# K and V of two heads in one transfer, and batches of eight heads, in a decode-attention block on one core

## The chip, the core and the metric

The kernel runs on one core of a Trainium2 chip. A core has a matrix engine (TensorE, PE in the profile), a vector engine (VectorE, DVE), an activation engine (ScalarE, ACT), GpSimd (POOL), SyncE (SP), which here only issues transfers, and 16 DMA engines that move data between the chip's memory (HBM) and the on-chip buffer (SBUF). Matrix products land in PSUM, of which the kernel uses eight banks of 512 float32 columns on 128 partitions. The metric is the device time of one execution in microseconds; the median of three runs is compared.

## What is computed

One decode step of a transformer block: four sequences (B = 4), one new token each, width D = 576, 32 query heads over 16 heads of K and V (two query heads share one), head size 128, and a cache of 16,384 tokens of which only the last 4,096 are attended to. Everything is bfloat16.

```python
q = (layernorm(x) @ wq)                        # (4, 1, 32 heads, 128)
k = k_cache[:, :, Sk - W:, :]                  # (4, 16, 4096, 128), each head used by 2 query heads
v = v_cache[:, :, Sk - W:, :]
p = softmax(einsum("bhqd,bhkd->bhqk", q, k) * Dh ** -0.5)
h = x + einsum("bhqk,bhkd->bhqd", p, v).reshape(B, 1, Hq * Dh) @ wo
gate, up = layernorm(h) @ W_gate, layernorm(h) @ W_up      # 576 x 4608 each
out = h + (gate * (gate > 0) * up) @ W_down                # 4608 x 576
```

The windows of K and V are 4 x 16 x 1 MB each, 134 MB together; the weights (wq, wo, gate, up, down) are some 25 MB.

## The kernel before

The work of each engine is written out by hand as a list of instructions, one list per engine, and the lists are tied together by semaphores (a small class, `Sched`, counts them). `S.op` and `S.dma` first wait for the named events in `deps` and then issue, so an engine never overtakes its own list. The unit of the attention part is one head of K and V of one sequence, 64 in all, numbered i.

**Transfers.** `prog_sync` is SyncE's list: it goes through `transfers` in order, waits until the target is free, and issues. The order is wq (five transfers), then K(i) with V(i - 5) behind it, then wo, gate and up, down, and last the output. K and V are 1 MB each. A head's window of 4,096 tokens is laid out as 128 rows of 32 consecutive tokens, one row of 8,192 bytes for each partition:

```python
return cache[b, kvh, SK - WIN:SK, :].rearrange("(p t) d -> p (t d)", p=128)
```

They go into slots of `pool`: a ring of six for K (`add_K`, the transfer at line 200) and of ten for V (`add_V`, line 203). A K slot comes free when VectorE has transposed that head (event TR), a V slot when PE has done its PV matmuls.

**Scores.** VectorE transposes each K head with 32 x 32 blocks (`tr`, line 382) from the slot into one of three `kT` buffers. PE's `qk(i)` then does eight matmuls of 512 columns into two PSUM banks; its weights `qz` hold q for the four heads of a batch in such a way that the four heads accumulate into different rows of the same two banks. Batches (four heads, 16 of them) alternate between two pairs of banks, so the scores are double-buffered.

**Softmax of a batch.** VectorE takes the row maxima (`rmax`, lines 385 and 387), GpSimd combines them over the partitions (PARTITION_ALL_REDUCE, line 268), VectorE makes the bias (`fbias`, lines 392 and 394), ScalarE takes the exponential with sums (line 314), VectorE transposes the result (`trp`, line 398), and ScalarE casts it into `prob` (line 321). In VectorE's list, `fbias` and `trp` of a batch stand behind the first and second transposes of the next batch.

**PV.** `pv(j)` is six heads behind `qk` in PE's list: eight matmuls of 512 columns with eight weight columns (four token groups times two query heads). After four heads ScalarE copies the bank out (`cpy`, line 301), and PE's `ext` picks the wanted blocks with four small matmuls. `norm` divides by the sums once for each sequence.

**The rest.** The output projection with wo, the second layernorm, gate and up, and down follow as the weights land; the wo transfers reuse K slots, gate and up V slots, and the down weights wait for the end of the output projection. All matmuls are recorded by one helper at line 469 (`mm`), so they share that line in the profile.

Of the kernel before, what the change touches and what calls it, by code (L numbers as in the profile page):

```python
# [19 lines left out]
T = WIN // 128  # L20
# [3 lines left out]
NPAIR = B * KVH  # L24
NB = 4
NBATCH = NPAIR // NB
# [3 lines left out]
SLOT = 4608  # L30
NKS = 6
NVS = 10
NSLOT = NKS + NVS
# [3 lines left out]
PVLAG = 6  # L37
# [63 lines left out]
def bass_sequential_preLN__sliding_block_cached__glu_gated_reglu__decode_kernel(  # L101
# [12 lines left out]
    with ExitStack() as es:  # L114
# [4 lines left out]

        pool = sb("pool", [128, NSLOT, SLOT], BF16)  # L120
        kT = sb("kT", [128, NKT, WIN // 2], FP32)
# [20 lines left out]
        mask = sb("mask", [128, 4, 2 * NB], FP32)  # L142
        selT = sb("selT", [128, 4, 2 * NB], FP32)
        rmx = sb("rmx", [128, 2], FP32)
        pmax = sb("pmax", [128, 2, 2 * NB], FP32)
        bcm = sb("bcm", [128, 2, 2 * NB], FP32)
        t8 = sb("t8", [128, 2 * NB], FP32)
        bias = sb("bias", [128, 2], FP32)
        rs2 = sb("rs2", [128, 2, 2], FP32)
# [3 lines left out]
        prob = sb("prob", [128, 3, NB, T, 2], BF16)  # L153
# [13 lines left out]
        sc = [es.enter_context(nc.psum_tensor(f"sc{i}", [128, 1024], FP32)) for i in range(2)]  # L167
        pb = [sc[0][:, 0:512], sc[0][:, 512:1024], sc[1][:, 0:512], sc[1][:, 512:1024]]
# [7 lines left out]

        rings = {"K": [list(range(NKS)), 0], "V": [list(range(NKS, NSLOT)), 0]}
        slot_user = {}
        transfers = []
        slot_of = {}  # L180

        def add(name, ring, consumer, make, fixed=None):
            if ring is not None:
                slots, i = rings[ring]
                s = slots[i % len(slots)]
                rings[ring][1] += 1
                free = slot_user.get(s)
                slot_user[s] = consumer
                key = f"slot{s}"
            else:  # L190
                s, free, key = fixed, None, "fix_" + str(name).replace("'", "").replace("(", "").replace(")", "").replace(", ", "_")
            slot_of[name] = s
            transfers.append((name, key, free, lambda e, s=s: make(e, s)))

        def kv(cache, i):
            b, kvh = divmod(i, KVH)
            return cache[b, kvh, SK - WIN:SK, :].rearrange("(p t) d -> p (t d)", p=128)

        def add_K(i):
            add(("K", i), "K", ("TR", i), lambda e, s: e.dma_start(out=pool[:, s, 0:WIN], in_=kv(A_k_cache, i)))  # L200

        def add_V(i):
            add(("V", i), "V", ("PV", i), lambda e, s: e.dma_start(out=pool[:, s, 0:WIN], in_=kv(A_v_cache, i)))

        for c in range(4):
            add(("wq", c), "V", "QMM", lambda e, s, c=c: e.dma_start(out=pool[:, s, 0:H * DH], in_=A_wq[c * 128:(c + 1) * 128, :]))
        add(("wq", 4), "V", "QMM", lambda e, s: e.dma_start(out=pool[:, s, 0:H * DH // 2],
                                                            in_=A_wq[512:576, :].rearrange("r (u n) -> (r u) n", u=2)))
        for m in range(NPAIR + VLEAD):
            if m < NPAIR:  # L210
                add_K(m)
            if m >= VLEAD:
                add_V(m - VLEAD)
        for g in range(NWO):
            add(("wo", g), "K", "ATTN",
                lambda e, s, g=g: e.dma_start(out=pool[:, s, :].rearrange("p (q x) -> p q x", q=2),  # L216
                                              in_=A_wo[g * 1024:(g + 1) * 1024, :].rearrange("(q p e) n -> p q (e n)", q=2, e=4)))
        for c in range(4):
            for kind, W in (("wg", B_W_gate), ("wu", B_W_up)):
                add((kind, c), "V", None,  # L220
                    lambda e, s, c=c, W=W: e.dma_start(out=pool[:, s, 0:F], in_=W[c * 128:(c + 1) * 128, :]))

        s4 = rings["V"][0][rings["V"][1] % NVS]
        for u, (kind, W) in enumerate((("wg", B_W_gate), ("wu", B_W_up))):
            transfers.append(((kind, 4), f"gu4_{u}", slot_user[s4],
                              lambda e, u=u, W=W: e.dma_start(out=pool[:, s4, u * HALF:(u + 1) * HALF],
                                                              in_=W[512:576, :].rearrange("r (u n) -> (r u) n", u=2))))
        wd_sb = pool[:, 0:NKS, :].rearrange("p s x -> p (s x)")[:, 0:FC * D].rearrange("p (g x) -> p g x", g=NG)
        WD = [(0, GD * JJ), (GD * JJ, 2 * GD * JJ)] + [(g * JJ, (g + 1) * JJ) for g in range(2 * GD, NG - 1)] + [(FC - JJ, FC - 1), (FC - 1, FC)]
        for k, (f0, f1) in enumerate(WD):  # L230
            g0, j0 = divmod(f0, JJ)
            g1, nj = (f1 // JJ, JJ) if f1 - f0 >= JJ else (g0 + 1, f1 - f0)
            transfers.append((("wd", k), f"wd{k}", "ATTN",
                              lambda e, g0=g0, g1=g1, j0=j0, nj=nj: e.dma_start(
                                  out=wd_sb[:, g0:g1, j0 * D:(j0 + nj) * D],
                                  in_=B_W_down[g0 * 128 * JJ:g1 * 128 * JJ, :].rearrange("(g p j) n -> p g (j n)", p=128, j=JJ)[:, :, j0 * D:(j0 + nj) * D])))
# [5 lines left out]
        def prog_sync(S):  # L242
            for name, key, free, make in transfers:
                S.dma("sync", make, key, deps=[free], name=land(name))
# [5 lines left out]
        def prog_pool(S):  # L250
# [12 lines left out]
                 deps=["P1"], name="IDF")  # L263
            for n in range(NBATCH):
# [7 lines left out]
        def prog_act(S):  # L272
# [12 lines left out]
            def qzero(n):  # L285
                b, q = divmod(n, 4)
                for g in range(4):
                    deps = []
                    if g == 0:
                        deps = ["D_QR", "QZ0"] if n < 2 else [("QK", NB * (n - 2) + NB - 1)]  # L290
                    src = bass.AP(tensor=qrep, offset=32 * g * 4 * H * B + 8 * q * B + b, ap=[[4 * H * B, 32], [2 * B, NB], [H * B, 4], [B, 2]])
# [13 lines left out]
            for n in range(NBATCH):  # L305
                for half in range(2):
                    deps = []
                    if half == 0:
# [5 lines left out]
                    S.op(a, lambda e, n=n, half=half: e.activation(  # L314
                        out=P[:, half * 512:(half + 1) * 512], in_=sc[n % 2][:, half * 512:(half + 1) * 512], func=ACT.Exp,
                        scale=SCALE, bias=bias[:, n % 2:n % 2 + 1], accum_out=rs2[:, n % 2, half:half + 1]),
                        deps=deps, name=("EXP", n) if half else None, signal=half == 1)
                deps = [("TRP", n)]
                if n >= 3:
                    deps.append(("PV", NB * (n - 3) + NB - 1))  # L320
                S.op(a, lambda e, n=n: e.copy(out=prob[:, n % 3, :, :, :],  # L321
                                              in_=probT[:, :, 0:2 * NB].rearrange("p t (r h) -> p r t h", h=2)), deps=deps, name=("CMP", n))
# [13 lines left out]
        def prog_dve(S):  # L336
# [17 lines left out]
            for x in range(2):  # L354
                S.op(v, lambda e, x=x: e.memset(pb[PVB + x], 0.0), name=f"PVZ{x}")  # L355
            S.op(v, lambda e: e.tensor_reduce(out=mask[:, 0, :], in_=ident_b[:, :].rearrange("p (r u) -> p u r", u=2 * NB), axis=AX.X, op=ALU.add),
                 name="M0")
            S.op(v, lambda e: e.tensor_reduce(out=mask[:, 3, :], in_=bass.AP(tensor=ident_b, offset=0, ap=[[128, 128], [1, 2 * NB], [32, 4]]),
                                              axis=AX.X, op=ALU.add), name="M3")
            S.op(v, lambda e: e.tensor_scalar(out=mask[:, 1, :], in0=mask[:, 0, :], scalar1=2 * BIG, scalar2=-BIG, op0=ALU.mult, op1=ALU.add),  # L360
                 deps=["M0"], name="M1")
            S.op(v, lambda e: e.tensor_scalar(out=mask[:, 2, :], in0=mask[:, 0, :], scalar1=-2 * BIG, scalar2=BIG, op0=ALU.mult, op1=ALU.add),
                 name="M2")
            S.op(v, lambda e: e.reciprocal(out=st1[:, 5:6], in_=st1[:, 4:5]), deps=["A_STD"], name="D5")
# [11 lines left out]
            def tr(i):  # L376
                deps = [land(("K", i))]
                if i >= NKT:
                    deps.append(("QK", i - NKT))
                src = pool[:, slot_of[("K", i)], 0:WIN].bitcast(FP32).rearrange("p (t c k) -> p c t k", c=2, k=32)  # L380
# [3 lines left out]
            def rmax(n):  # L384
                S.op(v, lambda e: e.tensor_reduce(out=rmx[:, n % 2:n % 2 + 1], in_=sc[n % 2][:, :], axis=AX.X, op=ALU.max),  # L385
                     deps=[("QK", NB * n + NB - 1)], name=("RMAX", n))
# [4 lines left out]
            def fbias(n):  # L391
                S.op(v, lambda e: e.scalar_tensor_tensor(out=t8[:, :], in0=bcm[:, n % 2, :], scalar=-SCALE, in1=mask[:, 2, :],  # L392
                                                         op0=ALU.mult, op1=ALU.max), deps=[("PAR", n)], name=("T8", n))
                S.op(v, lambda e: e.tensor_reduce(out=bias[:, n % 2:n % 2 + 1], in_=t8[:, :], axis=AX.X, op=ALU.min),  # L394
                     deps=[("T8", n)] + ([("EXP", n - 2)] if n >= 2 else []), name=("BIAS", n))

            def trp(n):
                S.op(v, lambda e: e.transpose(out=probT[:, :, :].rearrange("p t j -> p (t j)"), in_=P[:, :]),  # L398
                     deps=[("EXP", n)] + ([("CMP", n - 1)] if n >= 1 else []), name=("TRP", n))
                b, q = divmod(n, 4)  # L400
                S.op(v, lambda e: e.tensor_tensor(out=rs1[:, n % 2:n % 2 + 1], in0=rs2[:, n % 2, 0:1], in1=rs2[:, n % 2, 1:2], op=ALU.add),  # L401
                     name=("RS1", n))
                S.op(v, lambda e: e.tensor_scalar(out=rowsum[:, b, 8 * q:8 * q + 8], in0=mask[:, 3, :], scalar1=rs1[:, n % 2:n % 2 + 1],
                                                  scalar2=None, op0=ALU.mult), deps=[("RS1", n)], name=("RSUM", n))

            def norm(b):
# [3 lines left out]
                     deps=[("RS", b), ("EXT", 4 * b + 3)], name=("NORM", b))  # L410

            for i in range(NPAIR):
                tr(i)
                if i == 0:
                    S.op(v, lambda e: e.tensor_copy(out=qT_sb[:, :], in_=pb[QB][:, 0:H * B]), deps=["QMM"], name="D_QT")
                    S.op(v, lambda e: e.tensor_copy(out=qrep[:, :, :].rearrange("p c x -> p (c x)"), in_=pb[QR]), deps=["QREP"], name="D_QR")  # L416
                    S.op(v, lambda e: e.tensor_copy(out=selT[:, :, :].rearrange("p t (r h) -> p t r h", h=2),
# [224 lines left out]
```

## Time and profile before

| | |
|---|---|
| median of 3 runs | 389.65 us (389.43 to 389.69) |
| the profiled execution | 389.34 us, span 387.6 us |
| PE busy | 301.1 us, 78% of the span |
| VectorE (DVE) busy | 204.6 us, 53% |
| ScalarE (ACT) busy | 60.1 us, 16% |
| GpSimd (POOL) busy | 10.7 us, 3% |
| moved by the DMA queues | 159.88 MB, mean 413 GB/s |
| K transfers, issue to landing (median) | 26.1 us |
| V transfers, issue to landing (median) | 26.9 us |

The profile is one execution on the chip, recorded by hardware; its times are microseconds unless marked ns. The span is the time from the first to the last instruction. A page has a strip of 40 equal slices of the span, where a digit is the busy share in tenths; the row DMA is the mean over the 16 engines, and GB/s is what they moved. The queue lines give packets, megabytes and the share of 16 engines' span; the lines of issues give the tile and its source, the issuing queue, the number and size of the transfers and the median time from issue to landing. The chain that ended last follows the last instruction back to what released it. A group of instructions has its line, engine, operation, what it writes and reads, its shapes and its count; behind the first bar the busy time and the mean duration in ns, behind the second the idle time of the engine before them and what ended it.

### The profile page before, as it was taken

The page shows a single profiled execution, that of the slowest core. Times are in us where ns is not written, and L with a number is a line of the kernel's source. Part 1 is how long each engine was busy: PE and PEld are TensorE (multiplying, and loading weights), DVE is VectorE, ACT ScalarE, POOL GpSimd, SP SyncE. Part 2 cuts the span into 40 slices and gives each one's busy share as a digit, 9 for nine tenths or more (in the row PEclk, how much of TensorE's full clock was granted, in tenths as well). Part 3 has the DMA queues.
Part 4 walks back from the last instruction along what each step waited for, and adds up shares of the span by engine and source line. Part 5 has one row for each costly group of instructions (what it writes and reads, how often), then busy time and mean ns, then how long its engine had stood idle before and what let it go on. Part 6 is the DMA issues. An engine that isn't in the chain of part 4 may idle for free.

```text
span 387.6 us, 4471 instructions
## 1 busy us (share of the span) xinstructions
PE 301.1 (78%) x1906; PEld 131.3 (34%) x1906; DVE 204.6 (53%) x228; ACT 60.1 (16%) x173; POOL 10.7 (3%) x28
## 2 busy tenths in 40 slices
PE   0078779797979797979787878796879798774477
PEld 0053224242424242324232323242323233364344
DVE  0265967658483856574748575656566665011000
ACT  4020212111111111111111111111111111200000
POOL 3000000000000000000000000000000000000000
PEclk9999699999989998989999999899989989875559
DMA  8999999999999999999999999999999999999995
GB/s 322 419 419 423 423 421 418 420 423 420 423 419 420 424 421 422 420 420 421 421 424 421 418 424 421 424 417 421 421 421 422 423 421 419 414 418 421 418 412 203
DMA packets 23524, 159.88 MB, mean 413 GB/s; under 512 B 2505, under 2 KB 2641, under 8 KB 5585
## 3 DMA queue, kind: packets, MB, share of 16 engines
q1 hardware_dynamic: 23496, 159.59, 99.3%
q8 instruction: 15, 0.25, 0.3%
q14 instruction: 5, 0.03, 0.0%
q10 hardware_dynamic: 8, 0.00, 0.0%
HBM read 159.58 MB, written 0.00 MB: 412 GB/s over the span
## 4 chain that ended last, share of the span: by engine, by line
DMA 55%; PE 26%; DVE 12%; issue 4%; SPq 1%; ACT 0%; POOL 0%; POOLq 0%
DMA pool<-in_A_k_cache_dram 42%; PE sc L469 15%; PE pb L469 11%; DVE kT L382 8%; DMA pool<-in_B_W_down_dram 7%; DMA pool<-in_A_wo_dram 6%; DVE rmx L385 2%; SPq L216 1%; DVE pmax L387 0%; DVE pb L355 0%; ACT qz L294 0%; ACT xn_bf L281 0%; DVE sel L346 0%; PE pb L476 0%; DVE qrep L416 0%
## 5 line engine op out<-in xcount | busy, mean ns | idle before, releaser
L382 DVE STREAM_TRANSPOSE kT<-pool 128x2048 f32<-128x2048 f32 x64 | 147.2, 2305 | 59.5 <-DMA pool<-in_A_k_cache_dram 59.3
L469 PE MATMUL sc<-kT,qz 128*128 128x512 bf16 x512 | 137.8, 416 | 44.3 <-DVE t L392 33.0
L469 PE MATMUL pb<-pool,prob 128*8 128x512 bf16 x512 | 120.2, 393 | 0.0
L469 PEld LDWEIGHTS sc<-kT,qz 128*128 128x128 bf16 x512 | 47.0, 101 | 130.6 <-DVE t L392 40.5
L469 PEld LDWEIGHTS pb<-pool,prob 128*8 128x8 bf16 x512 | 38.9, 88 | 73.7 <-issue 28.2
L314 ACT ACTIVATE P<-sc,bias 128x512 f32<-128x512 f32 x32 | 21.7, 683 | 160.6 <-DVE bias L394 160.6
L385 DVE TENSOR_REDUCE rmx<-sc 128x1 f32<-128x1024 f32 x16 | 19.6, 1225 | 47.0 <-PE sc L469 47.0
L398 DVE STREAM_TRANSPOSE probT<-P 128x1024 f32<-128x1024 f32 x16 | 19.3, 1205 | 1.5 <-ACT P L314 1.5
L469 PEld LDWEIGHTS pb<-selT,cp 128*128 128x128 f32 x128 | 16.6, 191 | 6.6 <-ACT cp L301 4.2
L469 PE MATMUL pb<-selT,cp 128*128 128x8 f32 x128 | 15.4, 247 | 3.2 <-ACT cp L301 3.2
L301 ACT COPY cp<-pb 128x512 f32<-128x512 f32 x16 | 9.4, 586 | 53.5 <-PE pb L469 53.5
L469 PE MATMUL pb<-hnT,pool 128*128 128x4 bf16 x288 | 8.8, 167 | 9.8 <-DMA pool<-in_B_W_up_dram 5.2
L476 PE MATMUL pb<-ident_b,xn_bf 4*128 4x4 bf16 (+1 forms) x5 | 0.4, 175 | 19.6 <-ACT xn_bf L281 19.6
L294 ACT COPY qz<-qrep 32x32 bf16<-32x32 bf16 x64 | 13.9, 217 | 7.6 <-DVE qrep L416 7.0
L268 POOL PARTITION_ALL_REDUCE bcm<-pmax x16 | 5.9, 368 | 304.4 <-DVE pmax L387 304.4
L321 ACT CAST prob<-probT 128x256 bf16<-128x256 f32 x16 | 6.6, 414 | 44.6 <-DVE rs L401 44.6
L469 PEld LDWEIGHTS pb<-hnT,pool 128*128 128x128 bf16 x288 | 8.2, 104 | 10.3 <-DMA pool<-in_B_W_up_dram 5.4
L460 DVE TENSOR_TENSOR hhT<-pb,gate_sb 128x144 bf16<-128x144 f32 x1 | 0.3, 308 | 20.9 <-ACT gate_sb L330 20.9
L469 PE MATMUL pb<-pool,hhT 128*4 128x288 bf16 x72 | 10.0, 306 | 0.4 <-DMA pool<-in_B_W_down_dram 0.4
L469 PEld LDWEIGHTS pb<-pool,hhT 128*4 128x4 bf16 x72 | 6.3, 90 | 4.1 <-DMA pool<-in_B_W_down_dram 0.9
L469 PE MATMUL sc<-oX,pool 128*128 128x4 bf16 (+1 forms) x160 | 5.7, 170 | 1.6 <-DMA pool<-in_A_wo_dram 1.1
L476 PEld LDWEIGHTS pb<-ident_b,xn_bf 4*128 4x128 bf16 (+1 forms) x5 | 0.3, 107 | 19.6 <-ACT xn_bf L281 19.6
(93 smaller groups left out, 71.7 us busy)
## 6 DMA issues: line engine op xcount, KB each, us to landing
pool<-in_A_k_cache_dram SPq DMA_DIRECT2D x64, 1024.0 KB, 26.1
pool<-in_A_v_cache_dram SPq DMA_DIRECT2D x64, 1024.0 KB, 26.9
pool<-in_A_wo_dram SPq DMA_DIRECT2D x4, 1152.0 KB, 27.0
pool<-in_B_W_gate_dram SPq DMA_DIRECT2D x4, 1152.0 KB, 25.7
pool<-in_B_W_up_dram SPq DMA_DIRECT2D x4, 1152.0 KB, 24.4
pool<-in_A_wq_dram SPq DMA_DIRECT2D x4, 1024.0 KB, 7.9
pool<-in_B_W_down_dram SPq DMA_DIRECT2D x2, 1296.0 KB, 27.3
pool<-in_B_W_down_dram SPq DMA_DIRECT2D x5, 432.0 KB, 14.7
```

The source lines that it names most:

```text
L216: lambda e, s, g=g: e.dma_start(out=pool[:, s, :].rearrange("p (q x) -> p q x", q=2), in_=A_wo[g * 1024:(g + 1) * 1024, :].rearrange("(q p ...
L268: S.op(g, lambda e, n=n: e.partition_all_reduce(bcm[:, n % 2, :], pmax[:, n % 2, :], 128, bass_isa.ReduceOp.max), deps=deps, name=("PAR", n))
L294: S.op(a, lambda e, src=src, dst=dst: e.copy(out=dst, in_=src), deps=deps, name=("QZ", n) if g == 3 else None, signal=g == 3)
L301: S.op(a, lambda e: e.copy(out=cp[:, n % 2, :], in_=pb[PVB + n % 2]), deps=deps, name=("CP", n))
L314: S.op(a, lambda e, n=n, half=half: e.activation(out=P[:, half * 512:(half + 1) * 512], in_=sc[n % 2][:, half * 512:(half + 1) * 512], fun ...
L321: S.op(a, lambda e, n=n: e.copy(out=prob[:, n % 3, :, :, :], in_=probT[:, :, 0:2 * NB].rearrange("p t (r h) -> p r t h", h=2)), deps=deps, ...
L382: S.op(v, lambda e: e.transpose(out=dst, in_=src), deps=deps, name=("TR", i))
L385: S.op(v, lambda e: e.tensor_reduce(out=rmx[:, n % 2:n % 2 + 1], in_=sc[n % 2][:, :], axis=AX.X, op=ALU.max), deps=[("QK", NB * n + NB - 1 ...
L398: S.op(v, lambda e: e.transpose(out=probT[:, :, :].rearrange("p t j -> p (t j)"), in_=P[:, :]), deps=[("EXP", n)] + ([("CMP", n - 1)] if n ...
L460: S.op(v, lambda e: e.tensor_tensor(out=hhT[:, :, :], in0=pb[GUB][:, FC * B:2 * FC * B].rearrange("p (f b) -> p f b", b=B), in1=gate_sb[:, ...
L469: S.op(t, lambda e: e.matmul(o, lhsT=l, rhs=r, start=start, stop=stop, skip_group_check=skip), deps=deps, name=name, signal=name is not None)
L476: S.op(t, lambda e, c=c, w=w, src=src, base=base: e.transpose(out=tpv[0:w, base + c * 4:base + (c + 1) * 4], in_=src[0:B, c * 128:c * 128 ...
```

## The change

K and V of two neighbouring heads of one sequence (a "duo", 32 in all) travel in one transfer of 2 MB. The first head goes to partitions 0 to 63 and the second to partitions 64 to 127, each as 64 rows of 64 consecutive tokens, so a partition receives 16,384 bytes. K and V have four slots of 2 MB each; the weights are laid out over the same space by offset, and a transfer waits for every earlier user of its bytes.

A batch is eight heads (four duos), eight batches in all. Each duo is transposed in two halves (`tr(2d)`, `tr(2d + 1)`), and each half's scores hold both heads; one batch fills four banks, with no second set. QK of the next batch waits for the exponential of this one, two banks at a time. `fbias` now stands directly behind `rmax` in VectorE's list, and `trp` behind the first transpose of the next batch. A PV matmul serves both heads at once: its weights have sixteen columns, four for each token group, of which a partition of the first head holds zeros in the second head's two columns and the reverse; the zeros are written once by GpSimd, and the cast into `prob` is done in two halves of 64 partitions. PV runs five duos behind QK.

The core of the diff (renamed sizes, masks and the weights' index arithmetic are left out):

```diff
-T = WIN // 128
+T = WIN // 64
-NPAIR = B * KVH
+NDUO = B * KVH // 2
-SLOT = 4608
-NKS = 6
-NVS = 10
+DUO = 2 * WIN * DH // 128
+NKS = 4
+NVS = 4
 VLEAD = 5
-PVLAG = 6
+PVLAG = 5
...
-        pool = sb("pool", [128, NSLOT, SLOT], BF16)
-        kT = sb("kT", [128, NKT, WIN // 2], FP32)
+        pool = sb("pool", [128, (NKS + NVS) * DUO], BF16)
+        kT = sb("kT", [128, NKT, DUO // 4], FP32)
...
-        sc = [es.enter_context(nc.psum_tensor(f"sc{i}", [128, 1024], FP32)) for i in range(2)]
+        sc = es.enter_context(nc.psum_tensor("sc", [128, 2048], FP32))
...
-        def kv(cache, i):
-            b, kvh = divmod(i, KVH)
-            return cache[b, kvh, SK - WIN:SK, :].rearrange("(p t) d -> p (t d)", p=128)
+        def duo(cache, d):
+            b, m = divmod(d, KVH // 2)
+            return cache[b, 2 * m:2 * m + 2, SK - WIN:SK, :].rearrange("s (p t) d -> s p (t d)", p=64)
+
+        def add_K(d):
+            s = d % NKS
+            add(("K", d), f"kslot{s}", s * DUO, DUO, ("TR", 2 * d + 1),
+                lambda e, o: e.dma_start(out=o, in_=duo(A_k_cache, d)))
+
+        def add_V(d):
+            s = d % NVS
+            add(("V", d), f"vslot{s}", (NKS + s) * DUO, DUO, ("PV", d),
+                lambda e, o: e.dma_start(out=o, in_=duo(A_v_cache, d)))
...
+            S.op(g, lambda e: e.memset(prob[:, :, :, :, :].rearrange("p a r t x -> p (a r t x)"), 0.0), name="PZ")
...
-                S.op(a, lambda e, n=n: e.copy(out=prob[:, n % 3, :, :, :],
-                                              in_=probT[:, :, 0:2 * NB].rearrange("p t (r h) -> p r t h", h=2)), deps=deps, name=("CMP", n))
+                for s in range(2):
+                    S.op(a, lambda e, n=n, s=s: e.copy(out=prob[64 * s:64 * s + 64, n % 3, :, :, 2 * s:2 * s + 2],
+                                                       in_=probT[64 * s:64 * s + 64, :, 0:2 * NB].rearrange("p t (r h) -> p r t h", h=2)),
+                         deps=deps if s == 0 else [], name=("CMP", n) if s else None, signal=s == 1)
...
-                n, pos = divmod(i, NB)
-                if pos == NB - 1:
+                n, pos = divmod(i, 2 * NB)
+                if pos == 2 * NB - 1:
                     rmax(n)
+                    fbias(n)
                 if pos == 0 and n >= 1:
-                    fbias(n - 1)
-                if pos == 1 and n >= 1:
                     trp(n - 1)
...
             def qk(i):
-                n, pr = divmod(i, NB)
+                d, th = divmod(i, 2)
+                n, r = divmod(d, NB)
...
-                if pr == 0:
-                    deps.append(("QZ", n))
-                    if n >= 2:
-                        deps.append(("EXP", n - 2))
+                if r == 0:
+                    if th == 0:
+                        deps.append(("QZ", n))
+                    if n >= 1:
+                        deps.append(("EXP", n - 1, th))
...
-                    mm(pb[PVB + n % 2][32 * pr:32 * pr + 8, :], prob[:, n % 3, pr, 4 * tg:4 * tg + 4, :].rearrange("p t h -> p (t h)"),
-                       pool[:, s, tg * 512:(tg + 1) * 512], tg == 0, last,
+                    mm(pb[PVB + n % 2][32 * r:32 * r + 16, :], prob[:, n % 3, r, 4 * tg:4 * tg + 4, :].rearrange("p t h -> p (t h)"),
+                       pool[:, x0 + tg * 512:x0 + (tg + 1) * 512], tg == 0, last,
```

## The prediction, made before the changed kernel ran

> **What bounds the kernel now.** I read the page's strip of 40 slices first, then the DMA queues, then the issues, then the chain that ended last. The strip says whether any engine's work can matter at all:
>
> ```profile
> PE   0078779797979797979787878796879798774477
> ...
> DVE  0265967658483856574748575656566665011000
> DMA  8999999999999999999999999999999999999995
> GB/s 322 419 419 423 423 421 418 420 423 420 423 419 420 424 421 422 420 420 421 421 424 421 418 424 421 424 417 421 421 421 422 423 421 419 414 418 421 418 412 203
> ```
>
> The 16 DMA engines are full from the second slice to the last but one, at some 421 GB/s, while PE and DVE have holes in every slice. The queue view tells what fills them, and the packets can be counted against the code:
>
> ```profile
> q1 hardware_dynamic: 23496, 159.59, 99.3%
> ...
> q10 hardware_dynamic: 8, 0.00, 0.0%
> ...
> pool<-in_A_k_cache_dram SPq DMA_DIRECT2D x64, 1024.0 KB, 26.1
> pool<-in_A_v_cache_dram SPq DMA_DIRECT2D x64, 1024.0 KB, 26.9
> ...
> x_bf<-in_A_x_dram ACTq DMA_DIRECT2D x1, 4.5 KB
> out_dram<-out_sb SPq DMA_DIRECT2D x1, 4.5 KB
> ```
>
> q1 (all of SyncE's transfers) has 23,496 packets. Data packets by the code, one per contiguous row piece: wq 640, K and V 128 x 128 = 16,384, wo 1,024, gate and up 1,280, down 1,664, the output 4; together 20,996. What is left, 2,500, are 4-byte completion packets: 156 transfers of 128 rows x 16, and 4 for the output of 4 rows. q10 holds the x load alone: 4 rows, 4 data packets, 4 completions. So a transfer whose outermost count is 128 runs on 16 engines, and one whose outermost count is 4 runs on 4. No transfer of this kernel departs from that.
>
> The q1 share is 99.3% of 387.6 us: 384.9 us of work for each of the 16 engines, with no gaps between transfers. The last view shows the end of the chain:
>
> ```profile
> 321.89 24.79 DMA pool<-in_A_wo_dram
> 346.73 1.55 PE sc L469 x40
> 348.29 26.91 DMA pool<-in_B_W_down_dram
> 375.24 10.06 PE pb L469 x72
> 385.33 0.45 DVE out_sb L462
> ```
>
> It hangs on transfers to the end (start, length, what ran); a full queue sets the time. Of the groups I need three, with their busy time (idle time behind the second bar):
>
> ```profile
> L382 DVE STREAM_TRANSPOSE kT<-pool 128x2048 f32<-128x2048 f32 x64 | 147.2, 2305 | 59.5 <-DMA pool<-in_A_k_cache_dram 59.3
> L469 PE MATMUL sc<-kT,qz 128*128 128x512 bf16 x512 | 137.8, 416 | 44.3 <-DVE t L392 33.0
> L469 PE MATMUL pb<-pool,prob 128*8 128x512 bf16 x512 | 120.2, 393 | 0.0
> ```
>
> A transpose of K takes 2.3 us and waits for K in all 59 us; a QK matmul takes 137.8 / 512 = 0.269 us of PE and a PV matmul 120.2 / 512 = 0.235, since they are pipelined. The profiled execution took 389.34 us, 0.3 below the median of 389.65; 4.5 us of it (389.34 - 384.9) are start, last matmuls and store.
>
> **Price of a packet.** The trace's records of single packets, sorted by size (most frequent, mean): 1,152 B 51, 51 ns; 4,096 B 159, 159; 8,192 B 309, 314.3; 9,216 B 347, 352.3. The most frequent values lie on a line, (347 - 51) / (9,216 - 1,152) = 0.0367 ns per byte, 27.2 GB/s for one engine. K and V now cost each engine 128 transfers x 8 packets x 0.3143 = 321.8 us.
>
> **The change, part by part.** *The rows.* 16,384 B is beyond every row of q1. On the line it is 347 + 7,168 x 0.0367 = 610 ns; twice the mean 8 KB packet is 628.6; without a fixed part it would be 601. I take 612, near the line, because the excess over it (314.3 against 309) arises with all 16 engines reading, which I do not expect here. Half as many transfers also save 64 x 9.5 ns of completions, 0.6 us.
>
> *The split over engines.* Before, both sides of a K or V transfer have 128 as their outermost count. After, the pool side is still 128 rows (the instruction carries 128x1x8192), but the cache side is written as two heads x 64 rows x 8,192 elements: a window of 4,096 tokens lies in a head of 16,384, so heads and rows do not merge, and the outermost count of that side is 2. The trace has no transfer whose two sides differ. The ends are: the 128 decides (16 engines, 512 packets each) or the 2 decides (2 engines, 4,096 packets each). Nearest is the x row, where a small outermost count gave that many engines though the bytes could have been cut finer; and a cut must fit both sides, which 16 does not for a side of 2. I take 2. Fewer than 2 no row suggests. Which two, the records do not say; the shape is the same each time, so I take the same pair for every K and V transfer, one after the other.
>
> The Trainium skill, "DMA: Bandwidth & Descriptors", section "Why a DMA increments its semaphore by 16 and not by 1", speaks against this change where the rows leave it open: the number of engines is the largest up to 16 that divides the slowest dimension of both sides, and on this queue they are the lowest-numbered ones. By it the sum is the one with 2 engines; by the other reading of the rows it is the 383 us of the first rival.
>
> The pair's sum: out go 321.8 and 0.6 us, in come 64 transfers x 64 packets x 0.612 = 2,506.8. 389.3 - 322.4 + 2,506.8 = 2,573.7 us. The weights keep their 63 us on these two engines (wq before K0; wo, gate, up and down behind the last V), since each needs its sixteenth from them.
>
> The same page, "Latency and other measured facts", reports rows 4 MiB apart at 103 GB/s instead of 214; the two heads here are 4 MiB apart, which no run here has shown to matter. The pair asks for 2 x 16,384 / 612 = 53.5 GB/s, so my estimate from that page adds nothing.
>
> *Buffers.* Four K and four V slots of 2 MB replace six and ten of 1 MB. K(m) waits for the second transpose of K(m-4), V(m-5) for PV(m-9); behind either stands all of SyncE's list, V behind K and the weights behind both. With 2 engines a pair of heads takes 2 x 64 x 0.612 = 78.3 us to load. Its work is two transposes (4.6 us), two QK (16 x 0.269 = 4.3) and one PV (16 x 0.235 = 3.8), so slots come free long before the queue runs dry: cost nothing, hidden under 78 us. At the end wo (11.6 us of an engine's packets) and the first of gate and up lie queued while the last PV, its copy and the norm run (some 10 us by their rows).
>
> *Batches of eight on four banks, zeros in the PV weights.* Scores are no longer double-buffered: QK of the next batch waits for EXP, and the reduce, PARTITION_ALL_REDUCE and bias sit in DVE's list ahead of the next transpose. PV keeps 512 matmuls of 512 columns (32 pairs x 16), now with 16 weight columns, half of them zero; 8 and 128 weight columns cost 0.235 and 0.269 us for the same 512 columns, so 16 lie between, and I take 0.235. The copy into prob becomes two, the 64 qz copies halve, and a memset on POOL stands once before the first all-reduce. All of it lies beside 313 us of transfer per batch: nothing. What it costs without that cover is the second rival.
>
> **Rivals.** *First, faster: the split follows the pool side's 128* (or moves from pair to pair, so that eight transfers in flight fill the chip's queue). Then 389.3 - 322.4 + 512 x p: with p between 0.610 and 0.6286, 379 to 389 us, 383 at 0.618 (the step from 8,192 to 9,216 B in the means). For it: destination rows are what 128 counts elsewhere; against: no row where one side is smaller.
>
> *Second, slower by little: 16 engines, and the batch's chain takes over.* Per eight heads PE has 64 x 0.269 + 64 x 0.235 + 1 = 33.2 us. After the last QK of a batch one PV (3.8) runs, while DVE needs 2.45 (reduce, twice 1.225), 0.23, some 0.6 for POOL, 0.3, and 2.3 for the transpose: 5.9, so PE idles 2.1. EXP (4 x 0.88) and the twice longer probT transpose then delay the second transpose to 12.2, QK being done at 8.0: 4.1 more. The chain then is 33.2 + 6.2 = 39.4 us a batch against 39.6 of transfers (64 x 0.618): a tie. It decides from 39.6 up, at 8 us for each 1 us of chain: at 40.4 the kernel is back at the time of before, at 41.1 it takes 395.
>
> *Third, a cut in between:* 4 engines give 66.9 + 2,048 x 0.612 = 1,320 us, 8 give 694.
>
> **How the numbers follow.** Two engines 0.92; the first rival 0.05, of which 0.04 beyond 0.2% (0.8 us, about what a measurement of this kernel can tell from no change) and 0.01 within it; the second 0.01; the third 0.02. Faster 0.04, same 0.01, slower 0.95. The forecast is 2,574 us. Its ends: 601 ns per packet gives 2,529, 628.6 gives 2,642; another 0.3 us between transfers, should two engines leave gaps that sixteen do not, adds 19. Range 2,525 to 2,665, which leaves out the rivals and little else.
>
> **What would show it.** Right: the DMA row of the strip at 1 (2 of 16 engines) and GB/s near 53 nearly throughout, rising at both ends; completions of 2 for each K and V transfer, so q1 at some 8,192 + 4,612 data packets plus 128 + 452; 16 KB packets near 612 ns; PE idle over nine tenths, DVE waiting on K. Wrong: GB/s above 400 (first or second rival; PE without holes would mean the second), a strip at 2 to 5 (third), or 16 KB packets far off 0.61 us, which would move the time in proportion.

## The result, and the profile after

The changed kernel takes 2,574.22 us (median of 6 runs, 2,573.88 to 2,574.91) against 389.67 us before: 6.606 times as long, 95% interval 6.597 to 6.614. The forecast was 2,574. The profiled execution has a span of 2,573.0 us. These are the rows of its strip of 40 slices that were shown of before:

```profile
PE   1011011011111110121110120111111211101115
...
DVE  1011001100011000110010100100001100010000
...
DMA  2111111111111111111111111111111111111146
GB/s 115 54 54 54 54 54 54 54 54 54 54 54 54 54 54 54 54 54 54 54 54 54 54 54 54 54 53 54 54 54 54 54 54 54 54 54 54 54 110 267
```

No compute engine is busy for long. The DMA row stands at 1, as 2 of 16 engines would make it (0.125), and the rate is 53 to 54 GB/s, twice the 27.2 of one engine, from the second slice to the last but two. Only the weights at both ends move faster. The queue view and the issues:

```profile
q1 hardware_dynamic: 13384, 159.59, 15.1%
...
pool<-in_A_k_cache_dram SPq DMA_DIRECT2D x32, 2048.0 KB
pool<-in_A_v_cache_dram SPq DMA_DIRECT2D x32, 2048.0 KB
```

The bytes are those of before. Data packets are 8,192 of 16 KB for K and V and 4,612 others; the remaining 580 are completions: 452 of the other transfers and 128, two for each of 64 K and V transfers. Who waited for whom (total, times, longest):

```profile
DVE kT L397 <- DMA pool<-in_A_k_cache_dram: 2041.4, 32, 73.4
...
PE pb L482 <- DMA pool<-in_A_v_cache_dram: 990.1, 32, 40.9
```

VectorE, which waited 59 us for K before, now waits 2,041, once for each duo, up to 73 us. The chain that ended last puts these waits under another name:

```profile
another core or an unknown queue 87%; DVE 6%; PE 4%; issue 2%; DMA 1%; POOL 0%; ACT 0%; SPq 0%; POOLq 0%
```

The label only says that the view did not match these landings to their transfers; the waits above show that it is K and V.

### The profile page after: what moved, and what is told of

It is laid out like the page before. It is cut to its first block, busy times and chain, and to the rows that moved or that the text cites. A ratio compares the mean times of both kernels' runs of the same rounds, so it can differ in the third digit from the quotient of the medians.

```text
span 2573.0 us, 4160 instructions
## 1 busy us (share of the span) xinstructions
PE 408.3 (16%) x1827; PEld 156.3 (6%) x1842; DVE 200.2 (8%) x174; ACT 52.8 (2%) x133; POOL 10.5 (0%) x21
## 4 chain that ended last, share of the span: by engine, by line
another core or an unknown queue 87%; DVE 6%; PE 4%; issue 2%; DMA 1%; POOL 0%; ACT 0%; SPq 0%; POOLq 0%
DVE kT L397 4%; PE sc L482 2%; PE pb L482 2%; DMA pool<-in_B_W_down_dram 1%; DVE rmx L400 1%; DVE probT L413 1%; DVE sel L356 0%; POOL bcm L273 0%; DVE pmax L402 0%; DVE rowsum L418 0%; DVE t L407 0%; DVE bias L409 0%; ACT cp L307 0%; DVE rs_sb L422 0%
## 5 line engine op out<-in xcount | busy, mean ns | idle before, releaser
L482 PE MATMUL sc<-kT,qz 128*128 128x512 bf16 x497 | 184.1, 543 | 1105.0 <-DVE kT L397 1102.6
L482 PE MATMUL pb<-pool,prob 128*16 128x512 bf16 x512 | 182.0, 534 | 990.1 <-DMA pool<-in_A_v_cache_dram 990.1
L482 PEld LDWEIGHTS sc<-kT,qz 128*128 128x128 bf16 x512 | 61.7, 127 | 1225.2 <-DVE kT L397 1119.2
L482 PEld LDWEIGHTS pb<-pool,prob 128*16 128x16 bf16 x512 | 57.4, 117 | 1113.7 <-DMA pool<-in_A_v_cache_dram 974.4
L400 DVE TENSOR_REDUCE rmx<-sc 128x1 f32<-128x2048 f32 x8 | 18.3, 2291 | 29.2 <-PE sc L482 29.2
L330 ACT CAST prob<-probT 64x512 bf16<-64x512 f32 x16 | 10.2, 638 | 439.2 <-DVE rs L416 439.1
L413 DVE STREAM_TRANSPOSE probT<-P 128x2048 f32<-128x2048 f32 x8 | 18.2, 2274 | 2.9 <-ACT P L320 2.9
L482 PEld LDWEIGHTS pb<-selT,cp 128*128 128x128 f32 x64 | 8.2, 191 | 3.4 <-ACT cp L307 2.4
L482 PE MATMUL pb<-selT,cp 128*128 128x16 f32 x64 | 7.9, 255 | 1.4 <-ACT cp L307 1.4
L300 ACT COPY qz<-qrep 32x32 bf16<-32x32 bf16 x32 | 7.0, 219 | 36.6 <-DVE qrep L431 36.1
```

The lines of the kernel that those rows point to most:

```text
L300: S.op(a, lambda e, src=src, dst=dst: e.copy(out=dst, in_=src), deps=deps, name=("QZ", n) if g == 3 else None, signal=g == 3)
L330: S.op(a, lambda e, n=n, s=s: e.copy(out=prob[64 * s:64 * s + 64, n % 3, :, :, 2 * s:2 * s + 2], in_=probT[64 * s:64 * s + 64, :, 0:2 * NB ...
L482: S.op(t, lambda e: e.matmul(o, lhsT=l, rhs=r, start=start, stop=stop, skip_group_check=skip), deps=deps, name=name, signal=name is not None)
```

## The experiments

Theory: the cache side's outermost count of 2 puts every K and V transfer on the same two engines. Rival A: the 2 MB transfers, the 16 KB packets or the batches of eight cost the time. Rival B: reading two heads that lie 4 MiB apart does.

**The two halves as transfers of their own** (`e1_two_halves`):

```diff
+            transfers.append((name, key, free, [lambda e, s=s: make(e, pool[64 * s:64 * s + 64, off:off + n], s) for s in range(2)]
...
-            return cache[b, 2 * m:2 * m + 2, SK - WIN:SK, :].rearrange("s (p t) d -> s p (t d)", p=64)
+            return cache[b, 2 * m + s, SK - WIN:SK, :].rearrange("(p t) d -> p (t d)", p=64)
```

> The changed kernel with each 2 MB transfer issued as two of 1 MB, one for each head (64 rows of 16,384 bytes, both sides with 64 as outermost count); batches, buffers, packets as in the change. Theory (the outermost count of 2 puts K and V on 2 engines): 16 engines again, q1 with 16 completions for each transfer, the DMA row of the strip at 9, and 383 us if the transfers set the time (389.3 - 321.8 + 512 x 0.618), up to 395 if the batch's chain on PE does. Rival A (packets of 16 KB, or batches of eight on four banks, cost the time): stays above 2,000 us, since both are still there.

Measured: 692.2 us (686.7 to 697.7). The two engines are gone, but the expected 383 was missed:

```profile
DMA  9999999999999999999999999999999999999997
GB/s 311 214 216 215 214 211 214 218 214 213 214 215 217 214 212 215 219 214 212 214 217 217 212 215 216 217 212 214 219 214 215 215 219 214 216 219 215 418 417 308
...
q1 hardware_dynamic: 15304, 159.59, 99.7%
```

Of 15,304 packets 2,500 are completions, 16 for each 128-row or 64-row transfer; all 16 engines count as busy, and yet they move 214 GB/s. The packet records say how: 16 KB took 1,227 ns in the mean, twice 611. So the packets and the batches of rival A fall as the cause of the 2,574 us (both are still there), and a second limit appears that was not in the prediction. It is taken up below.

**One transfer, rows outside** (`e2_rows_outside`): the same bytes, packets and 2 MB, with the two dimensions of the cache side exchanged.

```diff
-            return cache[b, 2 * m:2 * m + 2, SK - WIN:SK, :].rearrange("s (p t) d -> s p (t d)", p=64)
+            return cache[b, 2 * m:2 * m + 2, SK - WIN:SK, :].rearrange("s (p t) d -> p s (t d)", p=64)
```

> The changed kernel with one edit: the cache side of a K or V transfer is written with the 64 rows outside and the two heads inside, so its outermost count is 64 and not 2; still one transfer of 2 MB with packets of 16,384 bytes. The rows of the two heads alternate over the partitions and the arithmetic behind is left as it is, so it computes other products. Theory (outermost count): 16 engines, 383 to 395 us as for the two halves. Rival A (size of transfer or packet, batches) and rival B (reading two heads 4 MiB apart in one transfer): stays near 2,574 us.

Measured: 386.9 us, 0.993 of before (0.9915 to 0.9949). The order of two dimensions carries the whole loss; rivals A and B fall together, since each transfer still has 2 MB and two heads that lie 4 MiB apart.

```profile
DMA  7999999999999999999999999999999999999993
GB/s 316 431 423 415 386 428 432 426 430 426 430 425 428 428 432 421 425 433 432 421 423 433 433 418 427 432 435 423 421 430 435 425 421 428 407 420 421 415 415 129
...
q1 hardware_dynamic: 14280, 159.59, 98.3%
```

1,476 completions are 452 + 64 x 16, and the rate lies near 428 GB/s where it was 421 before.

**The cut alone, in the kernel before** (`e4_before_cut2`): 1 MB transfers, 8 KB packets, batches of four.

```diff
-            return cache[b, kvh, SK - WIN:SK, :].rearrange("(p t) d -> p (t d)", p=128)
+            return bass.AP(tensor=cache.tensor, offset=((b * KVH + kvh) * SK + SK - 129 * 32) * DH,
+                           ap=[[65 * 4096, 2], [4096, 64], [1, 4096]])
```

> The kernel before with one edit: each head's 1 MB is read as 2 blocks of 64 rows with one row of 8 KB skipped between them (other rows than the reference by up to two rows). Packets of 8 KB, transfers of 1 MB, batches of four, slots as before. Theory: 2 engines, 128 transfers x 64 packets = 8,192 packets each at 0.309: 67.5 + 2,531 = 2,599 us, so the cut alone gives the whole loss. Rival A and rival B: 385 to 395 us.

Measured: 2,599.0 us, as expected to the microsecond:

```profile
GB/s 115 53 54 53 53 53 54 53 53 53 53 54 53 53 53 54 53 53 53 54 53 53 53 54 53 53 53 53 54 53 53 53 54 53 53 53 54 53 98 277
...
q1 hardware_dynamic: 21704, 159.59, 15.0%
```

Besides the 20,996 data packets there are 708 = 452 + 128 x 2 completions. The count of 2 gives the loss without any other part of the change.

**Four blocks** (`e3_cut4`; in the changed kernel, blocks a row apart):

```diff
-            return cache[b, 2 * m:2 * m + 2, SK - WIN:SK, :].rearrange("s (p t) d -> s p (t d)", p=64)
+            return bass.AP(tensor=cache.tensor, offset=((b * KVH + 2 * m) * SK + SK - WIN) * DH,
+                           ap=[[33 * 8192, 4], [8192, 32], [1, 8192]])
```

> The changed kernel with the cache side cut into 4 blocks of 32 rows, one row of 16 KB skipped between blocks so that they do not merge (it reads somewhat other rows than the reference, all near each other; nothing is 4 MiB apart). Theory: 4 engines, 2,048 packets each: 66.9 + 2,048 x 0.611 = 1,318 us, strip at 2 to 3, GB/s near 107, 4 completions for each transfer. Rival B (the 4 MiB between the heads): gone here, so 383 to 395 us. Rival A: near 2,574 us.

Measured: 1,348.4 us, 30 us over the expected 1,318:

```profile
GB/s 178 81 108 108 107 107 107 108 108 108 107 107 108 109 107 108 107 108 108 108 108 107 107 108 109 107 108 107 107 109 108 108 107 108 108 108 126 162 303 244
...
q1 hardware_dynamic: 13512, 159.59, 29.2%
```

There are 708 = 452 + 64 x 4 completions, and the rate is 107 to 109 GB/s, four times 27. Four engines it is. Most of the 30 us lies in the packets: 5,879 of the 8,192 took 611 ns, but from the first start to the last end they need 1,276.4 us, 25 more than 2,048 x 0.611. Of the 248 that took over 650 ns, 161 fall into the first 64 us of K and V, where the strip shows 81 GB/s, and 85 into the last 64 us, where weights move beside them. Why the first ones are slow no run shows.

**Two heads in 2 MB, rows of 8 KB** (`e9_before_2mb`): the kernel before, with its head layout, and a pair of heads in one transfer (V goes four heads behind K, not five).

```diff
-            return cache[b, kvh, SK - WIN:SK, :].rearrange("(p t) d -> p (t d)", p=128)
+            return cache[b, kvh:kvh + 2, SK - WIN:SK, :].rearrange("s (p t) d -> p s (t d)", p=128)
...
+            transfers.append(([(kind, i), (kind, i + 1)], f"slot{s}", free,
+                              lambda e: e.dma_start(out=pool[:, s:s + 2, 0:WIN], in_=kv(cache, i))))
```

> The kernel before with two heads in one 2 MB transfer and nothing else: each head still lies on all 128 partitions as rows of 8,192 bytes, the transfer carries 128 x 2 x 4,096 on both sides, so the outermost count is 128. Theory (the loss comes from the count of 2, the later gain from the packets of 16 KB, not from 2 MB): 16 engines, packets as before at 0.314, 64 completions fewer on each engine, 0.6 us: 389.0 us, the same; up to 392 if six K slots, now three pairs, make the queue wait. Rival A (a transfer of 2 MB is itself what cost the time): above 600 us.

Measured: 389.42 us, 0.9995 of before (0.9986 to 1.0005). 2 MB alone neither costs nor brings anything. In the run with rows outside a packet of 16 KB took 617.5 ns in the mean, against 2 x 314.3 for two of 8 KB; the gain to 428 GB/s is put down to that.

**What halves the rate on 16 engines.** Three more runs were about the miss of the first. In the first of them each duo goes in three transfers (`e5_middle`):

```diff
+            transfers.append((name, key, free, [lambda e, p0=p0, p1=p1: make(e, pool[p0:p1, off:off + n], (p0, p1)) for p0, p1 in ((32, 96), (0, 32), (96, 128))]
...
+            return bass.AP(tensor=cache.tensor, offset=((b * KVH + 2 * m) * SK + SK - WIN) * DH + p0 * 8192,
+                           ap=[[8192, p1 - p0], [1, 8192]])
```

> The two halves took 692 us although each transfer had 16 completions and the DMA row stood at 9: packets of 16 KB took 1,227 ns, twice those of the other runs, and the rate was 214 GB/s. Theory C (64 partitions, 0 to 63 or 64 to 127, can be written at half the rate only, whichever engines write): here each 2 MB goes in three transfers, 64 rows to partitions 32 to 95 first, then 32 rows to 0 to 31 and 32 rows to 96 to 127 (it reads 128 rows in a stretch, so other rows than the reference). If the halves of the limit lie at partition 64, the middle one runs at full rate, 4 packets of 0.612 for each engine, the outer ones at half rate, 2 packets of 1.227 each: 2.45 + 4.91 = 7.36 us for a pair of heads instead of 9.8, so 66.9 + 64 x 7.36 = 538 us, and two groups of 16 KB packets, half near 612 and half near 1,227 ns. Rival D (a transfer of 1 MB or of 64 rows with 16 KB rows is slow wherever it goes): 692 us or more.

Measured: 640.9 us (634.0 and 647.7) instead of 538:

```profile
GB/s 365 230 246 231 234 219 229 231 243 235 241 239 237 239 235 232 237 233 237 233 236 239 245 250 250 244 248 258 257 252 246 242 242 250 246 246 331 422 413 170
...
q1 hardware_dynamic: 16328, 159.60, 98.9%
```

There are no two groups of packets: 132 of 8,192 took under 650 ns, the mean is 1,090, and most lie between 900 and 1,250. Theory C in the form that was tested (a transfer across partition 64 runs at full rate) fell; rival D, 692 us or more, did not hold exactly either.

The other two cut the cache side finer, with the same edit as for four blocks: `[[9 * 8192, 16], [8192, 8], [1, 8192]]` (`e7_cut16`) and `[[5 * 8192, 32], [8192, 4], [1, 8192]]` (`e8_cut32`).

> The cache side cut into 16 blocks of 8 rows, one row skipped between blocks (other rows than the reference). Theory (engines = outermost count, up to 16): 16 engines, 512 packets each, 383 to 392 us, 16 completions for each transfer. If the count were not what decides, it would stay near the 1,348 us of the cut in 4.

> The cut in 16 blocks of 8 rows ran on 16 engines and yet took 670 us, at some 225 GB/s, like the two halves. Theory C, sharpened: what halves the rate is which partitions the 16 engines write at one moment. One edit against that run: 32 blocks of 4 rows, one row skipped between blocks, so nearly the same reads, again 16 completions, but rows dealt to the engines in another way (as in the run with rows outside, whose outermost count was 64). Expected: 383 to 388 us, GB/s near 428, 16 KB packets at 611 to 620 ns. Rival D (blocks with gaps, or small blocks, read slowly): 650 us or more.

Measured: 670.1 us and 387.2 us. These are the strip's rates and the queue line of 16 blocks:

```profile
GB/s 328 219 220 220 220 215 223 214 230 235 236 236 236 237 235 236 236 233 233 234 227 229 226 229 222 224 222 226 222 223 222 222 225 222 222 223 278 421 415 215
...
q1 hardware_dynamic: 14280, 159.59, 99.0%
```

And the same rows of 32 blocks:

```profile
GB/s 320 429 430 344 386 430 428 431 428 424 425 428 432 428 428 427 425 428 430 430 428 425 428 427 428 432 427 425 428 427 430 430 425 427 406 420 422 415 414 121
...
q1 hardware_dynamic: 14280, 159.59, 97.9%
```

The queue counts the same packets in both, 1,476 completions among them, so both use 16 engines on 128 partitions. In the middle one runs at 214 to 237 GB/s and the other near 428. Sixteen engines are needed for the full rate, and they are not enough.

The Trainium skill, "SBUF — State Buffer", section "Door 1: The DMA port swizzle (why `[64,N]` ≈ `[32,N]`)", offers a cause: partitions 0 to 63 reach only 8 of the 16 ports on SBUF's DMA side, and 64 to 127 only the other 8. The two halves' 214 GB/s, half of 428, agree with it. For the 16 blocks it would need the engines to fall on the same half of the ports at the same moments; the records here name neither engine nor partition of a packet, so this stays an inference. A conflict on the reading side is not excluded for the 16 blocks, whose reads differ a little from those of 32; against it for the two halves speaks that they read 1 MB in a stretch, as the kernel before does at 421. The cause of the half rate stays open.

**A version faster than both** (`e6_rows_right`): rows outside, and the arithmetic fitted to heads that alternate over the partitions. The exchange of the two dimensions is that of the second run; the rest is shown in part.

```diff
-                                  ap=[[4 * H * B, 32], [4 * B, NB], [H * B, 4], [B, 2]])
+                                  ap=[[4 * H * B, 32], [4 * B, NB], [H * B, 4], [B, 4]])
...
-                    S.op(a, lambda e, n=n, s=s: e.copy(out=prob[64 * s:64 * s + 64, n % 3, :, :, 2 * s:2 * s + 2],
-                                                       in_=probT[64 * s:64 * s + 64, :, 0:2 * NB].rearrange("p t (r h) -> p r t h", h=2)),
+                    S.op(a, lambda e, n=n, s=s: e.activation(out=prob[:, n % 3, :, :, 2 * s:2 * s + 2],
+                                                       in_=probT[:, :, 0:NHB].rearrange("p t (r s h) -> p s r t h", s=2, h=2)[:, s, :, :, :],
+                                                       func=ACT.Copy, scale=par[:, s:s + 1]),
...
+                S.op(v, lambda e: e.tensor_reduce(out=rs2[:, n % 2, 0:2], in_=P[:, :].rearrange("p (x e) -> p e x", e=2), axis=AX.X, op=ALU.add),
+                     deps=[("EXP", n, 1)], name=("PSUM2", n))
```

> Rows outside and heads inside as in the run before with 386.9 us, and the arithmetic fitted to it: heads alternate over the partitions, so the score weights have four columns for a pair of heads, the zeros of the PV weights come from the cast with a factor of 0 or 1 for each partition, and the sums are taken by VectorE over every other column (8 more reductions of about 2.3 us, no accumulation in the exponentials). Theory (packets of 16 KB on 16 engines move at 428 GB/s instead of 421, and the batch's chain is nearly hidden): 385.5 to 388.5 us, faster than before. Rival E (the chain of a batch, 39.4 us by the prediction's rows against 39.6 of transfers, takes over with the added reductions): 390 to 400 us, PE without holes and GB/s below 415 in the middle.

Measured: 385.09 us, 0.988 of before (0.9865 to 0.9898): a small gain, but clear of the interval. Its windows (us; PE, PEld, DVE, ACT and POOL busy, clock, DMA share, GB/s) in the middle of the run:

```profile
120.00:160.00 40.00, 32.46 (x147) 13.19 (x146) 30.22 (x21) 7.68 (x15) 0.39 (x1) 1.00 1.01 427
160.00:200.00 40.00, 32.31 (x138) 12.65 (x139) 28.10 (x18) 6.61 (x13) 0.39 (x1) 0.96 1.01 428
200.00:240.00 40.00, 34.43 (x141) 12.99 (x140) 26.14 (x18) 5.27 (x11) 0.39 (x1) 0.89 1.01 428
```

PE has 5.6 to 7.7 us of holes in each 40, and the transfers run without a gap: rival E did not come. Nor did the prediction's second rival: the run with rows outside, which has the change's own batches, kept PE busy for 33 to 36 us of each 40 between 80 and 320 us and moved 426 to 430 GB/s.

## Why the prediction was right, point by point

**The split over engines** was the step that decided, and it held: 2 engines, shown by the 128 completions, and the same two each time. For that 54 GB/s speaks, and more directly the first two K transfers: both are issued by 11.4 us of the span, yet the first lands at 54.4 and the second at 93.4, 39 us later, where another pair could have moved it beside the first. The cut alone and the exchange of two dimensions show the count of 2 as the cause. The rule for the number of engines that the prediction took from the Trainium skill, "DMA: Bandwidth & Descriptors", section "Why a DMA increments its semaphore by 16 and not by 1", agrees with the completions of these runs: 2 at an outermost count of 2, 4 at 4, and 16 at 16, 32, 64 and 128.

**The price of a packet**: 612 ns was taken; 6,122 of 8,192 took 611, the mean is 615.1. Successive packets of one engine start 611.5 ns apart in the mean, so their records overlap by some 4 ns. 4,096 x 0.6115 = 2,505 us against 2,506.8. The reason given for leaving out the excess, that it arises with 16 engines, holds only in part: the mean still lies 4 ns over the most frequent value here, and 6.5 ns over it with 16 engines (617.5, rows outside).

**Start and end**: the first 16 KB packet begins at 14.9 us of the span and the last ends at 2,519.9, which is the 2,505 between. The 53 us behind it are the weights on the pair (50 by the records of before) and the store. The two engines' list never ran dry, as the buffers' part had it. That the forecast came within 1 us is partly luck: the transfers were 1.8 us shorter than the sum's, and all the rest of the profiled execution (2,574.8 us) took 69.8 us instead of 66.9. Against a range of 140 us both are small.

**What was off without harm.** PE is idle for 84% of the span and not for over nine tenths. The granted clock fell from 0.916 to 0.577, and matmuls of the same 512 columns kept PE longer: 184.1 us for 497 recorded QK matmuls is 0.370 us each instead of 0.269, 182.0 for 512 PV matmuls 0.355 instead of 0.235. The work of a duo was thus larger than the sum's, and still far below the 78 us that hide it.

**The rivals' prices.** The first rival's 383 us for 16 engines was 2 to 4 us low: 386.9, 387.2 and, with the arithmetic fitted, 385.1. The packet was right (617.5 against 618), but the queue's share fell to 97.9 to 98.6% of the span, where the sum kept the 99.3% of before. The third rival's 1,320 us for 4 engines was measured as 1,348. What the prediction lacked is that 16 engines can also run at half the rate or little more, and take 641 to 692 us: a time that its third rival gives to 8 engines (694).

## What to carry to other kernels

Before you merge transfers, look at the outermost count of both sides of the access pattern, not at bytes or descriptors: here a 2 in front cost a factor of 6.6, and exchanging two dimensions of the same transfer gave it back and 0.7% more (1.2% with the arithmetic that fits). Count the completions, the packets of the profile's queue line less the data packets; they tell how many engines each transfer uses. And check the rate too, since 16 completions at 214 GB/s look just as busy in the strip as 16 at 428.

## What was not expected of the hardware

- A transfer of 64 rows to partitions 0 to 63 or 64 to 127, and one of 16 blocks of 8 rows, hold 16 engines at 99% busy and move some 214 and 225 GB/s. The recorded time of a 16 KB packet grows as the rate falls (1,227 and 1,162 ns in the mean against 611), so the busy share does not show it.
- With two engines SyncE's issues themselves were held up. In the timeline of the changed kernel (start, duration):

```profile
206.11 38.32 SPq L203 DMA_DIRECT2D pool<-in_A_k_cache_dram  x1
244.47 38.32 SPq L208 DMA_DIRECT2D pool<-in_A_v_cache_dram  x1
282.83 38.32 SPq L203 DMA_DIRECT2D pool<-in_A_k_cache_dram  x1
321.19 38.32 SPq L208 DMA_DIRECT2D pool<-in_A_v_cache_dram  x1
359.55 7.64 SPq L203 DMA_DIRECT2D pool<-in_A_k_cache_dram  x1
367.23 73.86 SPq L208 DMA_DIRECT2D pool<-in_A_v_cache_dram  x1
```

  Six of eight issues last 38.3 us and the other two 7.6 and 73.9. From the first V issue to the first of wo they follow one another every 39.0 us in the mean, about as long as one transfer takes (64 x 0.6115 = 39.1), where the median K issue before took 0.49 us. SyncE's list then runs at the pace of the engines; what holds an issue up, no run shows.
- The granted clock of TensorE went down with PE's busy share in these runs: 0.916 at 78% (before), 0.769 to 0.779 at 51 to 56% (the profiles of 634 to 698 us), 0.644 at 31% (four blocks) and 0.577 at 16% (the change).
